# One run of key-by-query products for two pairs of heads, on all four quarters of the array

## The chip, the cores and the metric

The program runs on one core of one Trainium2 chip. The metric is the device time of one execution in microseconds (us). Three runs of the kernel before gave 384.01, 384.09 and 385.25 us; the median is 384.09.

## What is computed

The reference has two stages. The first is a linear recurrence per head (batch 4, 8 heads, 768 steps, head size 48); the second is causal attention with four experts, of which each token takes the two with the highest gate:

```python
for t in range(S):                                  # per batch and head
    cur = einsum('bhd,bhe->bhde', u[None] * kt, vt)
    y[:, :, t] = einsum('bhd,bhde->bhe', rt, state + cur)
    state = wt[:, :, :, None] * state + einsum('bhd,bhe->bhde', kt, vt)
...
logits = x @ w_gate                                 # x: y of all heads, 768 x 384 per batch
topk = argpartition(-logits, K)[..., :K]            # K = 2 of E = 4
for e in range(E):
    q, k, v = x @ wq[e], x @ wk[e], x @ wv[e]       # head size 64
    a = softmax(causal(scale * q @ k.T))
    out += (weight of e) * (a @ v @ wo[e])
```

## The kernel before

The work is cut into eight units: a batch `b` and a half `g` of its 768 steps (names carry both digits: `xp01` is batch 0, second half). Each unit has a recurrence part (`rwkv`, L325) and an attention part (`moe`).

The recurrence part goes through the eight heads as four pairs (`p`, the third digit: `aps012`). A half has six chunks of 64 steps. Per pair, DVE scans the decays backward and forward inside the chunks (`suf` L382, `pre` L386); keys and queries are multiplied with the scans (`kt` L391, `pre` L393, on DVE or POOL). Then TensorE (PE) makes four kinds of runs, all products with fp32 operands:

- `ktp` (L421): three transposes of the weighted keys, copied out as `kts`.
- `ups` (L451, L452): what each chunk adds to the state, 12 products; DVE carries the state over the chunks in a scan (`ys` L459).
- `aps` (L437): keys by queries inside each chunk, 6 chunks x 2 heads = 12 products of 64 x 64. Head 0 lies in partitions 0 to 63, head 1 in 64 to 127, and each result goes to the same half of the partitions of one PSUM bank. So two of the four 64 x 64 quarters of the array are in use. DVE masks the result (`am` L440, one instruction on 128 partitions).
- `yps` (L481, L484): the output of the pair, from the state and from `am`, 24 products; DVE adds it to `xn` (`addy`, L490).

A product shows as two matmul records in the trace, so an `aps` run has 24 records and a `yps` run 48. The records of `ktp` are one per transpose.

When the four pairs of a unit are done, `xp` (L504) transposes `xn`, and `xh` and `xl` (L506, L508) split it into two fp32r parts. The attention part starts with the projections `pp` (L550), which wait for all three `xl` of the unit, then `vp` (L573), scores `sp` (L641), row maxima `mx` (L655), exponentials `a` (L657), transposes `tp` (L671), `yp` (L699) and `op` (L767).

All products of the recurrence use the PSUM tag `rw`, which has two banks: `ktp`, `aps` and `xp` take one, `ups` and `yps` both. The attention part has two banks `mo` and two double banks `sc`.

The order of the instructions is not the order of the code. Every step is an entry in a `Plan` with the engines that could do it, a cost, a due time and the tiles it needs; `Plan.order` puts the entries on the engines one by one, by due time and readiness, and the instructions are then issued in that order. Due times are positions in the unit plus a number per kind (tables `OFF` and `OFF0`, the latter for the first unit and the constants). In the beginning 94 filler products (`warm`, L816, bf16, result unused) stand in the order of PE: 14 at the very start, 80 wherever the plan saw PE without work. Constants for the masks are made on DVE (`masks`, L293); the weights are loaded and split into two parts by ACT and DVE (`weights`, L308).

Of the kernel before, what the change touches and what calls it, by code (L numbers as in the profile page):

```python
# [51 lines left out]
class Slot:  # L52
# [6 lines left out]
    def __call__(self):  # L59
# [14 lines left out]
BOTH = {"DVE": {"suf", "pre", "ys", "kt", "mr", "uk", "ur", "ux", "yl", "wsplit", "carry", "gate", "masks"},  # L74
        "POOL": {"kt", "mr", "uk", "ur", "ux", "gate", "g4", "wsplit"}}
# [132 lines left out]
def rwkv_moe(ctx: ExitStack, tc: tile.TileContext, wkr, vY, nat, uN,  # L208
# [99 lines left out]
    def weights(n, src, cols, parts=1):  # L308

        f = sb([128, cols], F32, "ATa", f"w_{n}")  # L310
        h = cst.tile([128, cols], F32R, name=f"wh_{n}")
        l = cst.tile([128, cols], F32R, name=f"wl_{n}")
        wts[n] = (h, l)
        load("wload", f, src, cols, [f])
        for c in range(parts):
            o = slice(c * cols // parts, (c + 1) * cols // parts)
            plan.add("wsplit", {"ACT": t_act(cols // parts) + 40}, lambda e, o=o: nc.scalar.copy(h[:, o], f()[:, o]),
                     [f], [("wh", n, c)])
            plan.add("wsplit", {"DVE": t_dve(cols // parts)}, lambda e, o=o: nc.vector.tensor_tensor(
                l[:, o], f()[:, o], h[:, o].bitcast(F32), op=ALU.subtract), [f, ("wh", n, c)], [("wl", n, c)])  # L320
# [4 lines left out]
    def rwkv(b, g, v0, v1):  # L325
# [9 lines left out]

        for p in range(NP):
# [88 lines left out]
            aps = bank("rw", f"aps{n}")  # L425

# [42 lines left out]
            yps = [bank("rw", f"yps{n}{h}") for h in range(2)]  # L469

            def outp(e, yps=yps, pre=pre, am=am, ys=ys, vy=vy):

                for i in range(3):
                    for part in range(2):
                        for h in range(2):
                            o = slice(i * D, (i + 1) * D)
                            r = slice(0, 64) if h == 0 else slice(64, 64 + D)
                            for q in range(2):
                                c = 2 * i + q
                                if part == 0:  # L480
                                    nc.tensor.matmul(yps[h]()[half(q), o], pre()[r, c, 0:C], ys()[r, :, c],  # L481
                                                     start=i == 0, stop=False)
                                else:
                                    nc.tensor.matmul(yps[h]()[half(q), o], am()[half(h), c, :], vy()[half(h), c, :],  # L484
                                                     start=False, stop=i == 2)
            plan.add("yps", {"PE": T_YPS}, outp, [pre, am, ys, vy], yps, mode="q", claim=[xn])

            for h in range(2):
                def addy(e, y=yps[h], o=slice((2 * p + h) * D, (2 * p + h + 1) * D)):
                    nc.vector.tensor_tensor(xn()[:, :, o], y()[:, 0:3 * D].rearrange("p (i e) -> p i e", i=3), xn()[:, :, o],  # L490
                                            op=ALU.add)
                plan.add("addy", {"DVE": t_dve(144)}, addy, [yps[h], (xn, p, h)], [(xn, p, h)])
# [27 lines left out]
    def moe(b, g, v0, v1):  # L520
# [95 lines left out]
        def scores(ep, i):  # L616
# [30 lines left out]
            plan.add("sc", {"PE": T_SC[3 * g + i]}, mm, [qh, ql, "masks"] + [(k, gg) for k in (kh, kl) for gg in range(g + 1)],  # L647
# [59 lines left out]
        def gather(i0, i1):  # L707
# [29 lines left out]
        def weigh(ep, yp, gT, i0, i1, yr, h, l):  # L737
# [9 lines left out]
            plan.add("gb", {"PE": 56 * (i1 - i0)}, mm, [gT], [gb], mode=GMODE[1])  # L747
# [62 lines left out]
    plan.add("masks", {"DVE": 2300}, masks, [], ["masks"])  # L810
# [25 lines left out]
BUFS = dict(lt=4, nat=3, ys=2, vy=3, suf=2, pre=3, am=2, kt=2, rk=2, kts=2, xn=2, xh=2, xl=2, lg=2, asum=2, ge=2, m1=2, rank=2, c1=1, c2=1,  # L836
            gs=2, mx=6, a=4, gg=2, gT=2, g3=2, yr=2, yh0=1, yh1=1, yl0=1, yl1=1, ob=3, v_sb0=1, v_sb1=1, ATa=3, ATb=2,
# [3 lines left out]
OFF = {'ld': -29.96, 'ldn': 1.58, 'ldv': -29.15, 'wload': 16.35, 'wsplit': 10.69, 'masks': -18.45, 'ldu': 21.72, 'uk': 21.36, 'ur': 6.66, 'rk': 1.63, 'ux': -0.38, 'ktp': 2.58, 'kts': -5.41, 'aps': 4.52, 'am': -13.64, 'ups': -2.03, 'us': -28.33, 'ys': -19.09, 'carry': 4.05, 'yps': -5.57, 'addy': 7.66, 'mr': -7.19, 'suf': 7.47, 'st': 3.45, 'yl': 18.34, 'wd': -16.55, 'xh': -22.56, 'yh': -0.23, 'ql': -3.54, 'ev': 7.02, 'pre': 0.41, 'g3': 12.57, 'warm': 1.65, 'ob': 3.25, 'lg': 3.18, 'sc': 0.35, 'yr': 32.73, 'xp': -3.54, 'gate': -0.08, 'inv': -0.13, 'gT': 14.31, 'y': -10.3, 'v': -2.96, 'exp': 10.79, 'op': 1.66, 'qd': 1.09, 'xl': -6.38, 'gp': -9.61, 'kt': -4.29, 'gb': -19.78, 'tp': 1.67, 'proj': -1.5, 'av': 3.07, 'vproj': 3.81, 'max': 8.92}  # L841
T_APS, T_UPS, T_YPS = 750, 395, 890
# [73 lines left out]
```

## Time and profile before

| | us |
|---|---|
| median of 3 runs | 384.09 |
| profiled execution | 385.41 |
| its span | 383.6 |
| PE busy | 370.9 |
| DVE busy | 314.0 |
| ACT busy | 230.7 |
| POOL busy | 150.3 |

The span runs from the first to the last instruction of the profiled execution; 1.8 us lie around it. Busy times are unions of records, and the filler products count as busy PE. On PE records overlap, so what a run of products takes is read from its start to the start of the next kind, not from the length of its records.

### The profile page before, as it was taken

Reading aid. Unit: us, or ns where it says so; the run is one execution under the profiler, and the core shown is the slowest. Engines: PE = TensorE matmul, PEld = TensorE weight load, DVE = VectorE, ACT = ScalarE, POOL = GpSimd, SP = SyncE. Lnnn points to the kernel's source line nnn. Section 1 sums busy time; section 2 is a strip of 40 time slices with the busy share of each in tenths; the row PEclk is TensorE's granted clock in tenths of the full one; section 3 lists DMA queues with packets and bytes.
Section 4 is the critical chain, followed back from the end, with each engine's and each line's share of the span. In section 5 each row is a group of like instructions: output and inputs, shape, how many; then the busy total and the mean of one; then the engine's idle time right before and its main releaser. Section 6 shows DMA issues by size and latency. Waiting matters only on the chain.

```text
span 383.6 us, 12786 instructions
## 1 busy us (share of the span) xinstructions
PE 370.9 (97%) x5259; PEld 287.9 (75%) x5259; DVE 314.0 (82%) x703; ACT 230.7 (60%) x646; POOL 150.3 (39%) x264
## 2 busy tenths in 40 slices
PE   8899999999999999999999999999999999999986
PEld 3555877778868778878878778788867868878765
DVE  7998998999899999989797988699896866347563
ACT  2563566746576767365766667447564745456653
POOL 4547647462425445526331465235641401001010
PEclk9999999999999999999999999999999999999999
DMA  7987264454424543644423343244321000101001
GB/s 252 367 271 228 72 209 157 136 179 144 153 63 142 158 141 100 224 117 139 131 69 113 123 129 94 95 137 146 95 63 48 17 3 23 41 3 64 0 2 62
DMA packets 18058, 45.18 MB, mean 118 GB/s; under 512 B 2000, under 2 KB 9424, under 8 KB 18000
## 3 DMA queue, kind: packets, MB, share of 16 engines
q1 hardware_dynamic: 18000, 44.37, 36.0%
q8 instruction: 41, 0.67, 0.7%
q14 instruction: 17, 0.14, 0.1%
HBM read 39.64 MB, written 4.72 MB: 116 GB/s over the span
## 4 chain that ended last, share of the span: by engine, by line
PE 75%; DVE 14%; ACT 4%; issue 2%; DMA 2%; POOL 1%; SPq 0%; ACTq 0%; DVEq 0%; POOLq 0%
PE pp L550 11%; PE tp L671 9%; PE yp L699 9%; PE sp L641 9%; PE op L767 7%; PE vp L573 7%; PE aps L437 6%; PE yps L481 4%; PE ups L451 2%; PE ktp L421 2%; DVE mx L655 2%; PE yps L484 2%; DVE suf L382 2%; PE warm L816 2%; ACT a L657 2%
## 5 line engine op out<-in xcount | busy, mean ns | idle before, releaser
L657 ACT ACTIVATE a<-sp,mx 128x128 f32<-128x128 f32 (+5 forms) x96 | 60.6, 635 | 29.5 <-DVE mx L655 22.9
L655 DVE TENSOR_REDUCE mx<-sp 128x1 f32<-128x128 f32 (+5 forms) x96 | 56.5, 615 | 14.5 <-PE sp L646 12.7
L671 PE MATMUL tp<-ident,a 128*128 128x128 f32 x336 | 56.3, 283 | 3.0 <-ACT a L657 1.4
L671 PEld LDWEIGHTS tp<-ident,a 128*128 128x128 f32 x336 | 37.6, 140 | 11.7 <-ACT a L657 3.2
L227 ACT COPY ATa<-tp 128x512 f32<-128x512 f32 (+3 forms) x66 | 32.2, 496 | 20.2 <-PE tp L671 19.7
L391 POOL TENSOR_TENSOR kt<-lt,suf 128x384 f32<-128x384 f32 x28 | 27.5, 981 | 42.9 <-PE aps L437 16.3
L398 POOL TENSOR_TENSOR nat<-nat,u_sb 128x288 f32<-128x288 f32 x30 | 28.9, 963 | 27.7 <-DMA nat<-in_nat_dram 19.7
L699 PE MATMUL yp<-ATa,v_sb 128*64 128x384 f32 (+2 forms) x240 | 38.3, 435 | 0.0
L550 PE MATMUL pp<-xh,wh_qk 128*128 128x384 f32 x96 | 37.1, 387 | 0.0
L411 ACT ACTIVATE xn<-nat,rk 128x48 f32<-128x48 f32 x117 | 29.9, 327 | 10.4 <-DVE rk L404 10.2
L382 DVE TENSOR_TENSOR_SCAN suf<-lt,one_suf 128x390 f32<-128x390 f32 x32 | 34.2, 1072 | 1.3 <-DMA lt<-in_wkr_dram 1.2
L386 DVE TENSOR_TENSOR_SCAN pre<-lt,inv_pre 128x390 f32<-128x390 f32 x32 | 33.4, 1045 | 0.2
L389 ACT COPY wdec<-suf 128x288 f32<-128x288 f32 x32 | 22.7, 711 | 17.5 <-DVE suf L382 11.4
L393 POOL TENSOR_TENSOR pre<-lt,pre 128x384 f32<-128x384 f32 x22 | 23.2, 1055 | 24.4 <-PE sp L646 9.1
L550 PE MATMUL pp<-xl,wh_qk 128*128 128x384 f32 x96 | 32.4, 338 | 0.0
L550 PE MATMUL pp<-xh,wl_qk 128*128 128x384 f32 x96 | 32.4, 337 | 0.0
L481 PE MATMUL yps<-ys,pre 64*64 64x48 f32 (+1 forms) x768 | 31.3, 262 | 0.9 <-DVE ys L459 0.6
L459 DVE TENSOR_TENSOR_SCAN ys<-ust,wdec 112x384 f32<-112x384 f32 x32 | 30.3, 951 | 2.1 <-ACT ust L227 1.3
L437 PEld LDWEIGHTS aps<-pre,kt 64*64 64x64 f32 x768 | 24.8, 134 | 7.0 <-issue 3.5
L437 PE MATMUL aps<-pre,kt 64*64 64x64 f32 x768 | 28.5, 221 | 1.3 <-DVE xn L490 0.5
L816 PE MATMUL warm<-one_suf 128*128 128x512 bf16 x94 | 27.1, 417 | 1.4 <-POOL one_suf L247 1.4
L481 PEld LDWEIGHTS yps<-ys,pre 64*64 64x64 f32 (+1 forms) x768 | 21.2, 133 | 9.5 <-issue 3.0
(136 smaller groups left out, 947.9 us busy)
## 6 DMA issues: line engine op xcount, KB each, us to landing
lt<-in_wkr_dram SPq DMA_DIRECT2D x31, 579.5 KB, 4.0
nat<-in_nat_dram SPq DMA_DIRECT2D x32, 432.0 KB, 3.9
vy<-in_vY_dram SPq DMA_DIRECT2D x32, 144.0 KB, 2.9
out_dram<-ob SPq DMA_DIRECT2D x24, 192.0 KB, 1.9
w_qk<-in_wqk_dram SPq DMA_DIRECT2D x1, 768.0 KB, 8.1
w_vg<-in_wvg_dram SPq DMA_DIRECT2D x1, 390.0 KB, 8.7
lt<-in_wkr_dram SPq DMA_DIRECT2D x1, 384.0 KB, 5.3
w_o<-in_wo_dram SPq DMA_DIRECT2D x1, 384.0 KB, 8.6
```

What stands on the lines that cost most here:

```text
L227: nc.scalar.copy(o, i)
L382: plan.add("suf", {"DVE": t_scan(WB)}, lambda e, suf=suf, w_=w_: nc.vector.tensor_tensor_scan(rev(suf()), rev(w_()), rev(one_suf), 0.0, op ...
L386: plan.add("pre", {"DVE": t_scan(WB)}, lambda e, pre=pre, w_=w_: nc.vector.tensor_tensor_scan(flat(pre()), w_()[:, 0:WB - 1], flat(inv_pre ...
L437: nc.tensor.matmul(a_[half(h), c * C:(c + 1) * C], k[half(h), c, :], m[half(h), c, 0:C], start=True, stop=True)
L481: nc.tensor.matmul(yps[h]()[half(q), o], pre()[r, c, 0:C], ys()[r, :, c], start=i == 0, stop=False)
L550: nc.tensor.matmul(pp()[:, 0:384], w[:, qk, k, cs], x()[:, k, :], start=(k == j == 0), stop=(k == j == 2))
L641: nc.tensor.matmul(spv(x)[:, h, :], q()[p, t], flat(k())[p, o], start=j == 0, stop=j == 2 and h < np_ - 1)
L655: plan.add("max", {"DVE": t_dve(n)}, lambda e, x=x, mx=mx: nc.vector.tensor_reduce(mx(), spv(x), axis=AX.XY, op=ALU.max, negate=True), [sp ...
L657: plan.add("exp", {"ACT": t_exp(n)}, lambda e, x=x, y=y, mx=mx, a=a: nc.scalar.activation(a()[:, 0:n].rearrange("p (a n) -> p a n", a=np_) ...
L671: nc.tensor.transpose(tp()[:, j * 128:(j + 1) * 128], a()[:, (j0 + j) * 128:(j0 + j + 1) * 128], ident)
L699: nc.tensor.matmul(yp()[e * 64:e * 64 + 64, lo:hi], v_sb[ep]()[:, j, e * 64:e * 64 + 64], at, start=(j == 0), stop=(j == nj - 1))
L816: plan.add("warm", {"PE": 216}, lambda e: nc.tensor.matmul(w()[:, 0:512], wz[:, 0:128], wz, start=True, stop=True), [], [w], want=1e6 if i ...
```

## The change

1. `aps` is no longer made per pair. Every second pair makes one run for itself and the pair before it: 24 products, 48 records. The first pair's heads go to their own half of the partitions of one bank, as before; the second pair's heads go to the other half of a second bank (`half(h ^ x)`), so all four quarters are named in turn.
2. The mask of the first pair is one DVE instruction on 128 partitions as before. That of the second pair is two on 64 partitions each, since it moves each half back to where its head belongs.
3. `yps` and `addy` of both pairs are entered after that (`finish`). `kt` and `pre` have four buffers now (2 and 3 before), `a` five (4 before).
4. In the beginning, `identb` and the four pieces of `idh` are made on ACT, `idh` is cleared on POOL, the rest of the masks stays on DVE. The weight splits have due times by matrix.
5. The plan's cost of an `aps` run, and all due times, are other numbers, so the order changes everywhere.

```diff
 def masks(e):
-    nc.vector.tensor_copy(identb, ident)
-    nc.vector.memset(idh, 0.0)
+    nc.scalar.copy(identb, ident)
     for a in range(2):
         for h in range(2):
             p = slice(64 * h, 64 * h + 64)
-            nc.vector.tensor_copy(idh[p, a, 64 * a:64 * a + 64], identb[p, 64 * h:64 * h + 64])
+            nc.scalar.copy(idh[p, a, 64 * a:64 * a + 64], ident[p, 64 * h:64 * h + 64])
+
+def masks2(e):
...
-def amat(e, aps=aps, kt=kt, pre=pre):
-    a_, k, m = aps(), kt(), pre()
-    for c in range(NH):
-        for h in range(2):
-            nc.tensor.matmul(a_[half(h), c * C:(c + 1) * C], k[half(h), c, :], m[half(h), c, 0:C],
-                             start=True, stop=True)
-plan.add("aps", {"PE": T_APS}, amat, [kt, pre], [aps], mode="q", claim=[am])
-plan.add("am", {"DVE": t_dve(384)}, lambda e, am=am, aps=aps: nc.vector.tensor_tensor(
-    am(), aps()[:, 0:NH * C].rearrange("p (c j) -> p c j", j=C),
-    dec_mask[:, None, :].to_broadcast([128, NH, C]), op=ALU.mult), [aps], [am])
...
+two.append((n, kt, pre, am, finish))
+if p % 2 == 0:
+    continue
+apss = [bank("rw", f"aps{t[0]}") for t in two]
+def amat(e, two=two, apss=apss):
+    for c in range(NH):
+        for h in range(2):
+            for x, (_, kt, pre, _, _) in enumerate(two):
+                nc.tensor.matmul(apss[x]()[half(h ^ x), c * C:(c + 1) * C], kt()[half(h), c, :], pre()[half(h), c, 0:C],
+                                 start=True, stop=True)
+plan.add("aps", {"PE": T_APS}, amat, [k for t in two for k in t[1:3]], apss, mode="q", claim=[t[3] for t in two])
+for x, (_, _, _, am, _) in enumerate(two):
+    for h in range(2) if x else (None,):
+        def mask(e, x=x, h=h, am=am, aps=apss[x]):
+            o = i = slice(0, 128)
+            if x:
+                o, i = half(h), half(1 - h)
+            nc.vector.tensor_tensor(am()[o], aps()[i, 0:NH * C].rearrange("p (c j) -> p c j", j=C),
+                                    dec_mask[i, None, :].to_broadcast([i.stop - i.start, NH, C]), op=ALU.mult)
+        plan.add("am", {"DVE": t_dve(384)}, mask, [apss[x]], [(am, h)])
+for t in two:
+    t[4]()
...
-T_APS, T_UPS, T_YPS = 750, 395, 890
+T_APS, T_UPS, T_YPS = 1100, 395, 890
```

What stands where, at the three places that the prediction speaks of. First PE, in the attention part of batch 0, first half, where the products `aps010` and `aps011` of the next unit are made. Before, `aps010` stands alone, and `aps011` follows 36 rows later:

```order
L646 LDWEIGHTS idh_99
L646 MATMUL sp00000_754<-causal_100,idh_99 128x128
L646 LDWEIGHTS idh_99
L646 MATMUL sp00000_754<-causal_100,idh_99 128x128
L437 MATMUL aps010_771<-pre010_711,kt010_685 64x64 x12
L573 MATMUL vp001_786<-wh_vg_112,xh00_453 128x260
L573 MATMUL vp001_786<-wl_vg_113,xh00_453 128x260
L573 MATMUL vp001_786<-wh_vg_112,xl00_462 128x260
L573 MATMUL vp001_786<-wh_vg_112,xh00_453 128x260
L573 MATMUL vp001_786<-wl_vg_113,xh00_453 128x260
L573 MATMUL vp001_786<-wh_vg_112,xl00_462 128x260
```

Now:

```order
L596 MATMUL vp000_789<-wh_vg_113,xl00_508 128x260
L596 MATMUL vp000_789<-wh_vg_113,xh00_500 128x260
L596 MATMUL vp000_789<-wl_vg_114,xh00_500 128x260
L596 MATMUL vp000_789<-wh_vg_113,xl00_508 128x260
L501 MATMUL aps010_800<-pre010_601,kt010_539 64x64
L501 MATMUL aps011_802<-pre011_691,kt011_688 64x64
L501 MATMUL aps010_800<-pre010_601,kt010_539 64x64
L501 MATMUL aps011_802<-pre011_691,kt011_688 64x64
L501 MATMUL aps010_800<-pre010_601,kt010_539 64x64
L501 MATMUL aps011_802<-pre011_691,kt011_688 64x64
```

Products of the two pairs now alternate, for 24 rows, and three products of `vp000` and nine of `vp001` stand between them and the first `yps010`.

Second DVE, the masks of the same two pairs. Before:

```order
L459 SCALAR_TENSOR_TENSOR ys010_784<-ust0_86,wdec0_80 112x384
L440 TENSOR_TENSOR am010_798<-aps010_771,dec_mask_96 128x384
L655 TENSOR_REDUCE mx0000_806<-sp00000_754 128x1
L655 TENSOR_REDUCE mx0010_808<-sp00000_754 128x1
L579 COPY lg00_752<-vp001_786 128x4
L382 SCALAR_TENSOR_TENSOR suf012_842<-lt012_455,one_suf_66 128x390
L490 TENSOR_TENSOR xn01_590<-yps0100_811,xn01_590 128x3x48
L490 TENSOR_TENSOR xn01_590<-yps0101_814,xn01_590 128x3x48
L384 RECIPROCAL inv_pre_69<-suf012_842 128x6
L655 TENSOR_REDUCE mx0001_877<-sp00010_848 128x1
L655 TENSOR_REDUCE mx0011_883<-sp00010_848 128x1
L440 TENSOR_TENSOR am011_892<-aps011_864,dec_mask_96 128x384
```

Now:

```order
L393 SCALAR_TENSOR_TENSOR pre012_780<-lt012_388,inv_pre_69 128x390
L453 SCALAR_TENSOR_TENSOR ys011_798<-ust1_88,wdec1_83 112x384
L585 TENSOR_TENSOR Kl00_826<-pp0001_742,Kh00_787 128x384
L510 TENSOR_TENSOR am010_832<-aps010_800,dec_mask_96 128x384
L510 TENSOR_TENSOR am011_844<-aps011_802,dec_mask_96 64x384 x2
L602 COPY lg00_856<-vp000_789 128x4
L408 TENSOR_TENSOR nat013_740<-nat013_740 128x288
L602 COPY lg00_856<-vp001_837 128x4
```

The one mask of `am010` is followed at once by the two of `am011`; before, `am011` stood ten rows later.

Third DVE, the end of the first unit's recurrence, where the last two `xl00` let the first projection start. Before:

```order
L319 TENSOR_TENSOR wl_vg_113<-w_vg_272,wh_vg_112 128x780
L490 TENSOR_TENSOR xn00_228<-yps0030_597,xn00_228 128x3x48
L490 TENSOR_TENSOR xn00_228<-yps0031_600,xn00_228 128x3x48
L319 TENSOR_TENSOR wl_o_115<-w_o_287,wh_o_114 128x768
L508 TENSOR_TENSOR xl00_462<-xp001_632,xh00_453 128x384
L508 TENSOR_TENSOR xl00_462<-xp002_636,xh00_453 128x384
L404 TENSOR_REDUCE rk011_655<-nat011_520 128x6
L413 TENSOR_TENSOR xn01_590<-nat011_520,rk011_655 128x3x48
L382 SCALAR_TENSOR_TENSOR suf010_668<-lt010_355,one_suf_66 128x390
L382 SCALAR_TENSOR_TENSOR suf011_677<-lt011_384,one_suf_66 128x390
```

Now:

```order
L389 SCALAR_TENSOR_TENSOR suf011_671<-lt011_370,one_suf_66 128x390
L486 TENSOR_TENSOR xn00_294<-yps0030_639,xn00_294 128x3x48
L486 TENSOR_TENSOR xn00_294<-yps0031_642,xn00_294 128x3x48
L391 RECIPROCAL inv_pre_69<-suf011_671 128x6
L398 TENSOR_TENSOR kt011_688<-lt011_370,suf011_671 128x384
L393 SCALAR_TENSOR_TENSOR pre011_691<-lt011_370,inv_pre_69 128x390
L531 TENSOR_TENSOR xl00_508<-xp001_677,xh00_500 128x384
L531 TENSOR_TENSOR xl00_508<-xp002_682,xh00_500 128x384
L411 TENSOR_REDUCE rk012_701<-nat012_530 128x6
L325 TENSOR_TENSOR wl_vg_114<-w_vg_277,wh_vg_113 128x780
```

Both scans of `011`, its `kt` and (further up) the scans of `010` have come ahead of the last two `xl00`; `wl_vg` and `wl_o`, the low parts of two weight matrices, have gone behind it. On PE all 94 fillers now stand ahead of the first `pp`; before, 8 of them stood behind it. The transposes `ktp010` and `ktp011` now stand ahead of it too, and did not before.

## Rows read from the trace of the kernel before

**Rows 1.** The page's part 1, busy time of each engine, and the chain's part by line.

```profile
PE 370.9 (97%) x5259; PEld 287.9 (75%) x5259; DVE 314.0 (82%) x703; ACT 230.7 (60%) x646; POOL 150.3 (39%) x264
...
PE pp L550 11%; PE tp L671 9%; PE yp L699 9%; PE sp L641 9%; PE op L767 7%; PE vp L573 7%; PE aps L437 6%; PE yps L481 4%; PE ups L451 2%; PE ktp L421 2%; DVE mx L655 2%; PE yps L484 2%; DVE suf L382 2%; PE warm L816 2%; ACT a L657 2%
```

**Rows 2.** Windows of the core: length, busy time of each engine with counts, granted clock, DMA.

```profile
core 0: us, PE busy (x) PEld busy (x) DVE busy (x) ACT busy (x) POOL busy (x), PEclk, DMA share, GB/s
0.00:38.29 38.29, 35.30 (x491) 19.28 (x492) 34.23 (x77) 17.13 (x44) 19.87 (x31) 1.00 0.82 280
100.00:140.00 40.00, 38.82 (x657) 29.12 (x650) 38.71 (x75) 27.02 (x73) 18.47 (x28) 1.00 0.44 134
60.00:180.00 120.00, 118.54 (x1898) 93.88 (x1896) 111.85 (x246) 77.34 (x224) 61.20 (x92) 1.00 0.46 140
38.29:383.60 345.31, 335.65 (x4770) 268.58 (x4768) 279.77 (x627) 213.53 (x602) 130.43 (x234) 1.00 0.32 100
```

**Rows 3.** Timeline of PE, two `aps` runs: start, length, line, tiles, count, idle before.

```profile
45.45 0.92 PE L437 MATMUL aps<-pre,kt 64*64 64x64 f32 x24
46.29 0.39 PE L573 MATMUL vp<-wh_vg,xh 128*128 128x260 f32 x1
...
174.89 1.61 PE L437 MATMUL aps<-pre,kt 64*64 64x64 f32 x48
176.43 0.39 PE L573 MATMUL vp<-wh_vg,xh 128*128 128x260 f32 x1
```

**Rows 4.** Timeline of PE, one `ups` run from first product to next kind.

```profile
44.20 0.25 PE L451 MATMUL ups<-nat,kts 64*64 64x48 f32 x1
...
44.72 0.33 PE L641 MATMUL sp<-Kh,Qh 64*128 64x128 f32 x2
```

**Rows 5.** Timeline of PE, one `yps` run from first product to next kind.

```profile
18.29 0.38 PE L481 MATMUL yps<-ys,pre 64*64 64x48 f32 x8
...
19.27 0.39 PE L816 MATMUL warm<-one_suf 128*128 128x512 bf16 x1
```

**Rows 6.** Timeline of PE, last fillers, first projection, one `ktp` run.

```profile
36.75 1.89 PE L816 MATMUL warm<-one_suf 128*128 128x512 bf16 x8
38.29 0.52 PE L550 MATMUL pp<-xh,wh_qk 128*128 128x384 f32 x1
...
41.89 0.52 PE L421 MATMUL ktp<-ident,kt 128*128 128x128 f32 x3
42.24 0.38 PE L816 MATMUL warm<-one_suf 128*128 128x512 bf16 x1
```

**Rows 7.** Timeline of DVE at the start: masks, first scans, one `am`.

```profile
3.45 0.23 DVE L294 CAST identb<-ident 128x128 bf16<-128x128 f32 x1
...
6.22 0.96 DVE L382 TENSOR_TENSOR_SCAN suf<-lt,one_suf 128x390 f32<-128x390 f32 x1
8.43 0.97 DVE L382 TENSOR_TENSOR_SCAN suf<-lt,one_suf 128x390 f32<-128x390 f32 x1 [1.25 <-DMA lt<-in_wkr_dram]
...
14.81 0.54 DVE L440 TENSOR_TENSOR am<-aps,dec_mask 128x384 f32<-128x384 f32 x1
15.28 0.56 DVE L401 TENSOR_TENSOR nat<-nat 128x288 f32<-128x288 f32 x1
```

**Rows 8.** Groups of DVE, 6.2 to 38.3 us: busy, mean ns, idle before.

```profile
L386 DVE TENSOR_TENSOR_SCAN pre<-lt,inv_pre 128x390 f32<-128x390 f32 x4 | 4.9, 1232 | 0.1
L382 DVE TENSOR_TENSOR_SCAN suf<-lt,one_suf 128x390 f32<-128x390 f32 x4 | 4.3, 1065 | 1.2 <-DMA lt<-in_wkr_dram 1.2
L319 DVE TENSOR_TENSOR wl_o<-w_o,wh_o 128x768 fp32r<-128x768 f32 x1 | 1.2, 1189 | 0.0
L319 DVE TENSOR_TENSOR wl_vg<-w_vg,wh_vg 128x780 fp32r<-128x780 f32 x1 | 1.0, 961 | 0.0
L384 DVE RECIPROCAL inv_pre<-suf 128x6 f32<-128x6 f32 x4 | 0.7, 175 | 0.0
```

**Rows 9.** Group of PE, line L437: busy, mean ns, idle before and what ended it.

```profile
L437 PE MATMUL aps<-pre,kt 64*64 64x64 f32 x768 | 28.5, 221 | 1.3 <-DVE xn L490 0.5 <-DVE pre L393 0.4 <-DVE ust L229 0.3
```

More of the change, by code (lines that the diff above doesn't have):

```diff
@@ L70 @@
          "SP": dict(PE=2000, DVE=2000, ACT=2000, POOL=2000, SP=2000)}
-BOTH = {"DVE": {"suf", "pre", "ys", "kt", "mr", "uk", "ur", "ux", "yl", "wsplit", "carry", "gate", "masks"},
-        "POOL": {"kt", "mr", "uk", "ur", "ux", "gate", "g4", "wsplit"}}
+BOTH = {"DVE": {"suf", "pre", "ys", "kt", "mr", "uk", "ur", "ux", "yl", "wsqk", "wsvg", "wso", "carry", "gate", "masks"},
+        "POOL": {"kt", "mr", "uk", "ur", "ux", "gate", "g4"}}
 class Plan:
@@ L316, in weights @@
             o = slice(c * cols // parts, (c + 1) * cols // parts)
[L317 removed]
+            plan.add("ws" + n, {"ACT": t_act(cols // parts) + 40}, lambda e, o=o: nc.scalar.copy(h[:, o], f()[:, o]),
                      [f], [("wh", n, c)])
[L319 removed]
+            plan.add("ws" + n, {"DVE": t_dve(cols // parts)}, lambda e, o=o: nc.vector.tensor_tensor(
                 l[:, o], f()[:, o], h[:, o].bitcast(F32), op=ALU.subtract), [f, ("wh", n, c)], [("wl", n, c)])
@@ L334, in prod @@
             return {"DVE": t_dve(cols), "POOL": t_pool(cols)} if first or FLEX else {"POOL": t_pool(cols)}
+        two = []
         for p in range(NP):
@@ L467, in rwkv @@
                          [], [ku + ("in",)])
[L469 to L492, printed above, removed]
+            def finish(p=p, n=n, pre=pre, am=am, ys=ys, vy=vy):
+                want(p / (NP + 1))
+                yps = [bank("rw", f"yps{n}{h}") for h in range(2)]
+                def outp(e, yps=yps, pre=pre, am=am, ys=ys, vy=vy):
+                    for i in range(3):
+                        for part in range(2):
+                            for h in range(2):
+                                o = slice(i * D, (i + 1) * D)
+                                r = slice(0, 64) if h == 0 else slice(64, 64 + D)
+                                for q in range(2):
+                                    c = 2 * i + q
+                                    if part == 0:
+                                        nc.tensor.matmul(yps[h]()[half(q), o], pre()[r, c, 0:C], ys()[r, :, c],
+                                                         start=i == 0, stop=False)
+                                    else:
+                                        nc.tensor.matmul(yps[h]()[half(q), o], am()[half(h), c, :], vy()[half(h), c, :],
+                                                         start=False, stop=i == 2)
+                plan.add("yps", {"PE": T_YPS}, outp, [pre, ys, vy] + [(am, h) for h in ((0, 1) if p % 2 else (None,))], yps, mode="q", claim=[xn])
+                for h in range(2):
+                    def addy(e, y=yps[h], o=slice((2 * p + h) * D, (2 * p + h + 1) * D)):
+                        nc.vector.tensor_tensor(xn()[:, :, o], y()[:, 0:3 * D].rearrange("p (i e) -> p i e", i=3), xn()[:, :, o],
+                                                op=ALU.add)
+                    plan.add("addy", {"DVE": t_dve(144)}, addy, [yps[h], (xn, p, h)], [(xn, p, h)])
@@ L494, in rwkv @@
+            for t in two:
+                t[4]()
+            two = []
         want(NP / (NP + 1))
@@ L646, in mm @@
                         nc.tensor.matmul(spv(x)[:, np_ - 1, w - 128:w], idh[p, a, :], causal[p, a, :], start=False, stop=a == 1)
-            plan.add("sc", {"PE": T_SC[3 * g + i]}, mm, [qh, ql, "masks"] + [(k, gg) for k in (kh, kl) for gg in range(g + 1)],
+            plan.add("sc", {"PE": T_SC[3 * g + i]}, mm, [qh, ql, "masks", "masks1"] + [(k, gg) for k in (kh, kl) for gg in range(g + 1)],
                      sps, mode="r")
@@ L809, in rwkv_moe @@
     plan.now = -1.0
-    plan.add("masks", {"DVE": 2300}, masks, [], ["masks"])
+    plan.add("masks", {"ACT": 600}, masks, [], ["masks1"])
+    plan.add("masks2", {"DVE": 1400}, masks2, [], ["masks"])
     plan.add("ldu", {"SP": 475}, lambda e: nc.sync.dma_start(
@@ L835 @@
 FLEX, LATE, SLACK = (True, True, 125)
-BUFS = dict(lt=4, nat=3, ys=2, vy=3, suf=2, pre=3, am=2, kt=2, rk=2, kts=2, xn=2, xh=2, xl=2, lg=2, asum=2, ge=2, m1=2, rank=2, c1=1, c2=1,
-            gs=2, mx=6, a=4, gg=2, gT=2, g3=2, yr=2, yh0=1, yh1=1, yl0=1, yl1=1, ob=3, v_sb0=1, v_sb1=1, ATa=3, ATb=2,
+BUFS = dict(lt=4, nat=3, ys=2, vy=3, suf=2, pre=4, am=2, kt=4, rk=2, kts=2, xn=2, xh=2, xl=2, lg=2, asum=2, ge=2, m1=2, rank=2, c1=1, c2=1,
+            gs=2, mx=6, a=5, gg=2, gT=2, g3=2, yr=2, yh0=1, yh1=1, yl0=1, yl1=1, ob=3, v_sb0=1, v_sb1=1, ATa=3, ATb=2,
             sc=2, mo=2, rw=2)
```

19 lines of the change are left out of this document (11 added, 8 removed).

## The prediction

> **What bounds the kernel now.** I read the page's busy times first, then the windows, then single runs on the timelines of PE and DVE. The page shows PE busy for 97% of the span and DVE for 82%, and the chain that ended last lies on PE for most of its length [rows 1]. That share would mislead in the first 38 us, where the fillers count as work, so the windows come next. From the first projection at 38.29 us [rows 6] to the end, PE is busy 335.65 of 345.31 us, and the granted clock is 1.00 there, its upper level of 2.4 GHz [rows 2]. Ahead of it DVE is the engine that has real work: 34.23 of 38.29 us, and of the 4.1 us that it idles 1.25 are one wait for data near the beginning [rows 2, 7]. DVE stays close behind afterwards: 93% from 60 to 180 us (111.85 of 120), 97% from 100 to 140 (38.71 of 40) [rows 2]. So there are two regimes. What DVE does ahead of the last `xl` of the first unit moves everything behind it; after that, a microsecond less of products on PE is a microsecond of time, as long as DVE keeps up.
>
> **The sum is made against the profiled execution**, 385.4 us with a span of 383.6; the median of the runs is 1.3 below it, and that is taken off at the end.
>
> **The fused runs.** An `aps` run alone occupies PE for 0.84 us (45.45 to 46.29); two back to back take 1.54 (174.89 to 176.43) [rows 3]. 28 of the 32 runs lie behind the first projection; by the order 20 stand alone and 8 in four adjacent pairs: 20 x 0.84 + 4 x 1.54 = 23.0 us. They become 14 runs of 48 records. No row shows such a run, so it is bounded. It can't be shorter than today's run, since each quarter still takes 12 records: 0.84. It has no reason to be longer than two back to back: 1.54. Two runs that already use four quarters lie between: `ups`, 24 records in 0.52 (44.20 to 44.72) [rows 4], is 1.04 for 48; `yps`, 48 records, takes 0.98 (18.29 to 19.27) [rows 5]. Both stream 48 columns per record where `aps` streams 64; if all of it grew with the columns, that would be 1.39 and 1.31. I take 1.1, above `yps` by part of the columns. 14 x 1.1 = 15.4, so PE is given back 7.6 us; with 0.84 it is 11.2, with 1.39 3.5.
>
> The `yps` run starts its 48 records 20 ns apart (0.98 / 48) [rows 5]. A rule of the Trainium skill says otherwise: "TensorE: Matmul & The Clock Gate" (section "Wait — 56ns, not 53.3ns?") states that products never start closer than about 25 ns apart. By it 48 records take at least 1.2 us, an estimate, and the gain is at most 6.2 us. The trace does not agree with it, and the sum keeps the 1.1.
>
> **The masks on DVE.** An `am` record is 0.54 long and the next starts 0.47 behind it [rows 7]. The second pair's mask becomes two instructions of as many columns each, so at 0.47 apiece 16 are added, 14 of them behind the first projection: 6.6 us on DVE. From 60 to 180 us some six fused runs fall (14 over the 286 us to the last `aps`). There PE could be done 6 x 0.54 = 3.2 us sooner (23.0 - 15.4 over 14 is 0.54 each), in 116.8; DVE would need 111.85 + 2.8 = 114.65, a share of 98%. The best that the trace shows is the 97% of 100 to 140 us, which makes it 118.4, or 1.6 lost again. With a little for waits at other places I put +2.5; it could be nothing, since DVE is at 81% over the whole of 38.29 to 383.6 [rows 2], or the 8 us of the first rival.
>
> **The start.** By the order, the first unit's DVE work up to its last `xl` gains two `suf`, two `pre`, two reciprocals, a `kt`, an `rk`, three products into `xn` and two more masks, and loses `wl_o`, `wl_vg` and a copy. By the mean records of that stretch [rows 8]: 2 x 1.07 + 2 x 1.23 for the scans, 3 x 0.47 for `kt` and two masks, about 0.3 each for the six narrower ones (an estimate between the 0.18 of a reciprocal and the 0.47 of a mask), together 7.8; off go 1.19 + 0.96 for the weights and 0.47 for the copy, 2.6. That is +5.2, less some 0.4 by which records overlap. DVE is idle for 4.1 us of the first 38.29 [rows 2], 1.25 of it for the second scan's transfer, the rest ahead of its first instruction and in short waits; more work at hand can fill one or two of these. I take +3.5, from 1 to 5: the first projection at about 41.8. Part comes back: two `ktp` of 0.35 each (41.89 to 42.24) [rows 6] are done by then, -0.7, and the 8 fillers that stood behind the first projection, at 0.19 each (36.75 to 38.29 for eight) [rows 6], are gone, -1.5. The scans done early relieve DVE by their 4.6 us between 38 and 60 us, which is why no wait is added there.
>
> **The other edits.** `identb` and `idh` leave DVE, but the first scan follows the masks at 6.22 and the second still waits until 8.43 for its transfer [rows 7], so they give 0.2 at most. On ACT and POOL they lie ahead of the first scan's result, which both engines need for their first work; without that cover five copies at the 0.23 of `identb` [rows 7] would cost 1.2. `wl_vg` is needed by `vp`, behind 18 projections; `wl_o` much later: nothing. SP issues the same transfers in nearly the same order; the third scan's decays have moved ahead of one `nat` and two smaller loads, worth something between -1 and +1 inside the start's range. `finish` puts `yps` behind both pairs: in the order at least eleven attention products stand between each fused run behind the start and its first `yps`, and more again ahead of the second, against one mask of 0.47 and then two; nothing as long as DVE's queue is not late by more than these products take.
>
> Sum: 385.4 - 7.6 + 2.5 + 3.5 - 0.7 - 1.5 - 0.2 = 381.4 for a profiled execution, 380.1 for the timed ones.
>
> **Rivals.**
>
> *The fused run waits for the second pair.* It needs `kt` and `pre` of two pairs and both `rw` banks at once, and what is behind it on PE is attention work that was ready. Until the last mask has read them, neither `ktp`, `ups`, `xp` nor `yps` gets a bank. For it: DVE at 93 to 97% makes `pre`, and a late scan would now stop PE where before it stopped a quarter of its work. Against it: all 32 runs together waited only 1.3 us before [rows 9], and `kt` and `pre` have more buffers. Each 0.1 us per run beyond my 2.5 costs 1.4; from 0.3 per run it decides and the gain is gone. At 0.6 per run, 8.4 us in place of the 2.5, the time is 386.0.
>
> *The quarters don't overlap.* Then the change does not do what it says: 14 x 1.54 = 21.6, a gain of 1.4 where I have 7.6, and as PE is no faster, DVE is not pressed (the 2.5 goes): 383.8. For it: in the new run two products that share rows of the array, and then two that write the same bank, follow each other at once. Against it: today's run has 24 records in 0.84, and they already send both row halves into one bank; `yps` has twice as many in 0.98 [rows 3, 5].
>
> "TensorEngine Tiling (Array Packing)" of the Trainium skill (Gotcha 1) has a rule that would bring this about: different row tiles cannot access the same PSUM bank at the same time. By it today's run of two quarters would gain nothing from the second; the rows of `aps` and `yps` above show no such halving, so I give it little.
>
> *All of it, and more.* The fused run takes the 0.98 of `yps` (gain 9.3), DVE is never late, and the start costs 2: 385.4 - 9.3 + 2 - 2.4 - 1.3 = 374.4. For it: PE waits little now, 9.7 us from 38.29 on with the tail included [rows 2]. Against it: the wider columns, and the 97% of DVE.
>
> **How the numbers follow.** My forecast, 377 to 383, gets 0.47; the third rival 0.20; the wait for the second pair 0.20; quarters that don't overlap 0.13. The likeliest is 380.1. A range from 374.4 to 386.5 holds all but the ends of the outer cases. What a measurement of this kernel can tell from no change is about 0.3%, 1.2 us. The forecast and the third rival are faster (0.67); half of the case of no overlap and a quarter of the waiting case come out within it (0.12); the rest is slower (0.21).
>
> **What would show it.** In the profile of the changed kernel: an `aps` run of 48 records of about 1.1 us from its start to the next kind (0.85 and 1.5 are the rivals' numbers); 48 `am` records with those on 64 partitions no shorter than 0.5; the first `pp` near 41.8 us; no `warm` behind it; DVE at 95% or more from 60 to 180 us; idle time ahead of the `aps` records of less than 3 us in all. The forecast is wrong if the first `pp` comes at 38 or 45, if PE's idle time behind it grows by more than 6 us, or if the granted clock falls below 1.00 in a pause between the last filler and the first projection, which no row of before shows.

## The result, and the profile after

The change is faster, by 1%: 380.96 us median against 384.40, ratio 0.9901, 95% interval [0.9878, 0.9924]. Predicted were 380.1, and 374.4 to 386.5. The execution that was profiled then was a disturbed one of 1098.69 us (the other three took 380.67 to 381.22), so the profile after, and what the experiments are compared with, is of the same kernel run again: median 381.93 (384.74 before), ratio 0.9932 [0.9915, 0.9948]; profiled 381.39, span 379.6. For a profiled execution the sum had 381.4.

Nearly the same number, but not from the same terms. First the page of after, its part 1 and the chain by line [rows 1], and the PE and DVE groups of the two edited steps (busy, mean ns, idle before) [rows 9]:

```profile
PE 361.6 (95%) x5259; PEld 280.8 (74%) x5259; DVE 319.7 (84%) x717; ACT 237.0 (62%) x662; POOL 136.0 (36%) x254
...
PE pp L573 12%; PE yp L722 10%; PE tp L694 10%; PE sp L664 8%; PE op L790 7%; PE vp L596 6%; PE yps L477 5%; DVE am L510 3%; DVE mx L678 3%; DVE ys L453 3%; PE ups L445 2%; PE ktp L428 2%; DMA nat<-in_nat_dram 2%; DVE pre L393 2%; ACT a L680 2%
...
L510 DVE TENSOR_TENSOR am<-aps,dec_mask 64x384 f32<-64x384 f32 (+1 forms) x48 | 26.5, 552 | 1.4 <-PE aps L501 0.7
```

```profile
L501 PE MATMUL aps<-pre,kt 64*64 64x64 f32 x768 | 15.0, 222 | 0.0
```

`aps` has left the chain's first lines and `am` has come in. PE gave back 9.3 us of busy time and the span got 4.0 shorter; the rest turned into idle time. The windows, with the columns of [rows 2]:

```profile
0.00:38.29 38.29, 34.33 (x488) 17.88 (x491) 34.16 (x72) 19.81 (x55) 17.46 (x31) 1.00 0.78 274
40.00:47.00 7.00, 5.86 (x42) 4.93 (x43) 5.96 (x13) 3.25 (x8) 2.20 (x3) 0.51 0.64 196
47.00:60.00 13.00, 13.00 (x249) 11.34 (x247) 11.94 (x28) 7.17 (x21) 7.77 (x10) 1.00 0.44 133
60.00:180.00 120.00, 116.11 (x1876) 93.03 (x1875) 114.11 (x256) 80.67 (x237) 59.52 (x98) 1.00 0.45 139
```

DVE (the third busy time) is at 95% from 60 to 180 us, from 93%, and PE fell from 118.54 to 116.11 there. And the second row has what before had nowhere: a granted clock of 0.51, the lower level (1.2 GHz), for seven microseconds.

The fused run in the steady part, on PE's timeline (start, length) [rows 3]: 48 records, and the next kind starts 0.86 us after the first.

```profile
99.84 0.93 PE L501 MATMUL aps<-pre,kt 64*64 64x64 f32 x48
100.70 0.66 PE L694 MATMUL tp<-ident,a 128*128 128x128 f32 x4
```

The start, on the same timeline [rows 6]: the last fillers, the idle time behind them, and the first projection, still at the lower clock.

```profile
36.86 0.61 PE L840 MATMUL warm<-one_suf 128*128 128x512 bf16 x2
...
40.60 1.54 PE L527 MATMUL xp<-ident,xn 128*128 128x128 f32 x6 [1.89 <-DVE xn L486]
42.69 0.90 PE L428 MATMUL ktp<-ident,kt 128*128 128x128 f32 x3 [0.54 <-DVE xl L531]
43.24 0.67 PE L573 MATMUL pp<-xh,wh_qk 128*128 128x384 f32 x1
```

To see where PE's time went, each record is counted from its start to the start of the next, less the idle time between (over 30 ns), and added up by kind. Profiled executions, us; E5, E9 and E10 are experiments, below:

| | before | after | E5 | E9 | E10 |
|---|---|---|---|---|---|
| `aps` | 26.6 | 14.0 | 14.1 | 25.7 | 25.6 |
| `yps` | 32.4 | 34.1 | 34.4 | 32.4 | 31.9 |
| `tp` | 43.7 | 45.8 | 46.0 | 44.9 | 44.8 |
| `vp` | 28.9 | 30.7 | 30.7 | 30.6 | 30.6 |
| all kinds | 370.7 | 361.3 | 361.1 | 369.8 | 369.5 |
| idle, in all | 7.8 | 13.2 | 11.2 | 6.9 | 5.1 |
| idle behind the first `pp` | 6.2 | 8.1 | 7.8 | 4.5 | 3.8 |

After against before: `aps` gave 12.6; idle time took 5.3 of it back, `tp` 2.1, `yps` and `vp` 1.8 each; `yp` and others gave 2.4 more.

### The profile page after: what moved, and what is told of

It reads as the page before. It is cut to its first block, busy times and chain, and to the rows that moved or that the text cites. A ratio compares the mean times of both kernels' runs of the same rounds, so it can differ in the third digit from the quotient of the medians.

```text
span 1096.9 us, 12800 instructions
## 1 busy us (share of the span) xinstructions
PE 1087.8 (99%) x5252; PEld 677.6 (62%) x5259; DVE 322.1 (29%) x717; ACT 241.1 (22%) x662; POOL 131.2 (12%) x254
## 4 chain that ended last, share of the span: by engine, by line
PE 99%; issue 0%; DVE 0%; POOL 0%; ACT 0%; POOLq 0%
PE pp L573 17%; PE tp L694 13%; PE yp L722 13%; PE sp L664 10%; PE vp L596 8%; PE op L790 8%; PE warm L840 8%; PE yps L477 4%; PE ktp L428 4%; PE aps L501 4%; PE yps L480 3%; PE xp L527 3%; PE sp L669 2%; PE ups L446 2%; PE ups L445 1%; PE gb L768 1%
## 5 line engine op out<-in xcount | busy, mean ns | idle before, releaser
L694 PE MATMUL tp<-ident,a 128*128 128x128 f32 x336 | 154.6, 650 | 0.0
L722 PE MATMUL yp<-ATa,v_sb 128*64 128x384 f32 (+2 forms) x240 | 120.6, 1221 | 0.0
L573 PE MATMUL pp<-xh,wh_qk 128*128 128x384 f32 x96 | 90.7, 945 | 0.0
L840 PE MATMUL warm<-one_suf 128*128 128x512 bf16 x87 | 85.2, 1235 | 5.3 <-issue 3.2
L573 PE MATMUL pp<-xl,wh_qk 128*128 128x384 f32 x96 | 84.6, 881 | 0.0
L573 PE MATMUL pp<-xh,wl_qk 128*128 128x384 f32 x96 | 83.8, 873 | 0.0
L480 PE MATMUL yps<-vy,am 64*64 64x48 f32 x768 | 55.7, 368 | 0.0
L480 PEld LDWEIGHTS yps<-vy,am 64*64 64x64 f32 x768 | 53.2, 337 | 0.0
L664 PE MATMUL sp<-Kl,Qh 64*128 64x384 f32 (+4 forms) x128 | 51.0, 796 | 0.0
L664 PE MATMUL sp<-Kh,Ql 64*128 64x384 f32 (+4 forms) x128 | 49.8, 777 | 0.0
```

The lines of the kernel that those rows point to most:

```text
L573: nc.tensor.matmul(pp()[:, 0:384], w[:, qk, k, cs], x()[:, k, :], start=(k == j == 0), stop=(k == j == 2))
L664: nc.tensor.matmul(spv(x)[:, h, :], q()[p, t], flat(k())[p, o], start=j == 0, stop=j == 2 and h < np_ - 1)
L694: nc.tensor.transpose(tp()[:, j * 128:(j + 1) * 128], a()[:, (j0 + j) * 128:(j0 + j + 1) * 128], ident)
L722: nc.tensor.matmul(yp()[e * 64:e * 64 + 64, lo:hi], v_sb[ep]()[:, j, e * 64:e * 64 + 64], at, start=(j == 0), stop=(j == nj - 1))
L840: plan.add("warm", {"PE": 216}, lambda e: nc.tensor.matmul(w()[:, 0:512], wz[:, 0:128], wz, start=True, stop=True), [], [w], want=1e6 if i ...
```

## Experiments

All run in the changed order, but for E6 and E7, and all with the kernel before beside them on the same chip. Its median lay between 384.55 and 384.78 on each of these chips, so the medians of different experiments are compared below.

**E1, two quarters.** Undoes the use of the quarters alone: both pairs' heads to their own halves, masks still 1 + 2.

```diff
-    nc.tensor.matmul(apss[x]()[half(h ^ x), ...
+    nc.tensor.matmul(apss[x]()[half(h), ...
...
-            o, i = half(h), half(1 - h)
+            o, i = half(h), half(h)
```

> The changed kernel in its own order, but the second pair's products go to the same halves as the first's, so that 48 records use two quarters instead of four; its two masks stay, on the half where the result now lies. If the four quarters overlap and PE is what counts: the run grows to about 1.5 us, 14 x 0.4 = +5 to +7 us, 386 to 388. If the quarters never overlapped: no change, 381. If DVE holds the pace in the first half: the run grows, but only half of it shows, +2 to +3.

Measured 385.93, ratio to before 1.0030 [1.0016, 1.0044]: 4.0 above the changed kernel, nearest to the first expectation and short of its 5 to 7. The run's length doubles; in the first unit it is 1.59 us from its start to the filler behind it:

```profile
32.33 1.66 PE L501 MATMUL aps<-pre,kt 64*64 64x64 f32 x48
33.92 0.82 PE L840 MATMUL warm<-one_suf 128*128 128x512 bf16 x3
```

So the four quarters work side by side, and they are worth 4.0 us of the end (E9 repeats this with the clock kept up), though they take 16 x 0.73 = 11.7 us off PE's runs. Without them, but with the split masks, the change as a whole would have gained nothing.

**E2, two quarters and one mask.** As E1, and the second pair's mask is one instruction on 128 partitions, which two quarters allow.

```diff
-        if x:
-            o, i = half(h), half(1 - h)
+        if x and h:
+            return
```

> As the kernel on two quarters, but the second pair's mask is one instruction on 128 partitions again (the other entry of the plan issues nothing): 16 masks of 0.47 less, 7.5 us of DVE. If DVE had reserve: within 1 us of the kernel on two quarters. If DVE holds the pace: 2.5 us or more below it.

Measured 382.87, ratio 0.9959 [0.9943, 0.9975]: 3.1 us below E1, for 16 masks fewer, as expected if DVE holds the pace. Not all of that need be the masks: the mean granted clock of an execution was 0.990 to 0.996 in E1 and 0.990 to 1.000 in E2. With the clock kept up it is 1.7 (E9, E10). The kernel of E2 is also 1.9 us below the kernel before, on two quarters and with as many masks; the changed kernel is only 0.9 below E2, and their intervals overlap. So more than half of the gain of 2.8 stands without the four quarters. Which of the other edits gives it (order, start, buffers) no run separates; the new tables alone do not (E6).

**E3, masks twice.** The changed kernel, each half mask of the second pair issued two times.

```diff
-        nc.vector.tensor_tensor(am()[o], ...
+        for _ in range(2 if x else 1):
+            nc.vector.tensor_tensor(am()[o], ...
```

> The changed kernel, with both masks of the second pair issued twice in a row: 32 instructions of 0.47 more, 15 us of DVE in the same order. If DVE is in reserve and only the beginning is bound by it: +1 us for the beginning and +1 to +3 behind it, 383 to 385. If DVE holds the pace up to 180 us: its share there is in excess of 98% already, so +6 to +9 us, 387 to 390.

Measured 400.96, ratio 1.0411 [1.0380, 1.0442], above both expectations: 19 us for 32 more masks, more than the 15 us that 32 steps of 0.47 put on DVE. Part of the 19 is the clock, which in this profile was at its lower level for 17.75 us in three stretches, against 7 in the changed kernel; at E5's 2.6 us for seven the 10.75 us more are worth some 4 us, an estimate:

```profile
42.50:49.50 7.00, 6.24 (x44) 5.31 (x45) 5.66 (x11) 3.06 (x9) 2.92 (x3) 0.51 0.65 211
73.25:80.25 7.00, 6.70 (x75) 4.94 (x77) 4.84 (x12) 3.57 (x13) 1.58 (x2) 0.51 0.17 44
162.00:165.75 3.75, 3.75 (x103) 3.25 (x96) 3.12 (x10) 2.71 (x10) 1.28 (x4) 0.54 0.17 46
```

The largest part is idle PE before records of one kind, put down to the masks (0.4 us there in the changed kernel):

```profile
L477 PE MATMUL yps<-ys,pre 48*64 48x48 f32 (+1 forms) x768 | 36.6, 265 | 11.7 <-DVE am L511 9.7 <-DVE xl L532 1.1 <-DVE xn L486 0.6
```

Most of it stands inside the runs, behind the fourth record: 12 of the 16 `yps` runs of a first pair stop there, so that the fifth record starts 0.39 to 1.67 us after the fourth. E12 shows why.

**E5, fillers.** The changed kernel with 13 more fillers in the first unit: 8 ahead of its second `xp`, 5 behind the third (`fill` issues that many).

```diff
...
+    fill(8 if k == 1 else 0)
     for i in range(3):
         nc.tensor.transpose(xp()[:, i * 128:(i + 1) * 128], ...
+    fill(5 if k == 2 else 0)
```

> The changed kernel with 13 more filler products of 512 columns in the first unit: eight ahead of its second triple of transposes and five behind the third, where TensorE stood idle for 1.9 and 0.5 us and the granted clock was 0.5 from 40.1 to 46.9 us. Theory A (the drop of the clock costs the start what its stretch at half the clock shows): the granted clock stays at 1.00 from 33 us on, the seventeen units of work of TensorE between 40 and 47 us end about 2 to 3 us sooner, and the kernel ends 2 to 3 us before 381.9, at 379 to 380. Theory B (behind 40 us VectorE is what TensorE waits for, so the clock is hidden): the clock stays up too, the idle time of TensorE between 41 and 60 us grows by as much as its work gets shorter, and the end moves by under 0.5 us. Theory C: the fillers themselves hold up the transposes by 0.2 us each time and the time rises by 0.5 us or more.

Measured 379.36, ratio 0.9858 [0.9846, 0.9871], 2.6 us below the changed kernel and the fastest of all. The clock stays at its upper level and PE is busy throughout, in the window that had 0.51:

```profile
40.00:47.00 7.00, 7.00 (x82) 5.42 (x81) 6.70 (x15) 4.36 (x11) 3.59 (x4) 1.00 0.65 213
```

The first projection comes 0.6 sooner (42.61), that of the second unit 2.0 (72.9 after 74.9), the end of the span 2.2: won by then and kept. Theory A.

**E6, new tables alone, and E7, old tables.** The kernel before with the changed offsets and start times; the changed kernel with those of before. Of the tables one line stands here, as E7 changes it; E6 does the opposite, and `OFF`, `OFF0` and `LEAD` go with it.

```diff
-T0, T1 = (18.33, 15.35)
+T0, T1 = (21.06, 16.77)
```

> The kernel before with the changed one's table of offsets and start times, and with its own products, masks and buffers. Theory A (the gain of the change is mostly the order that the new table gives, since two quarters with one mask came out 1.9 us below the kernel before): this one ends near 382.9, 1 to 2 us below the kernel before. Theory B (the table fits only the paired products): it ends at 384.5 or above. What it can't show is the start, because it keeps its constants on VectorE: first projection between 38 and 40 us.

> The changed kernel with the offsets and start times of the kernel before: the paired products on four quarters, split masks and ScalarE's constants alone. Theory A (most of the gain is the order): 384 us or above. Theory B (most of it is the paired products, 10.3 us of TensorE's work, whose worth does not hang on the table): 382 or below.

Measured 390.30, ratio 1.0144 [1.0127, 1.0160], and 389.27, ratio 1.0115 [1.0083, 1.0147]. Theory A of E6 and theory B of E7 both fall: the new tables gain nothing with the old products, nor the fused run with the old tables. E6's clock stayed up. E7's did not, so its 389.27 is not the price of the order alone:

```profile
38.75:49.25 10.50, 8.71 (x106) 7.40 (x98) 8.07 (x17) 5.56 (x16) 6.53 (x7) 0.51 0.43 126
72.75:80.00 7.25, 7.25 (x79) 4.55 (x79) 5.26 (x14) 4.88 (x18) 3.89 (x5) 0.53 0.41 125
```

In this execution (392.09) that is 10.75 us more at the lower level than in the changed kernel, again some 4 us by E5's price (an estimate); without them it would still be above the kernel before. That each table suits its own products also limits E1, E2, E9 and E10: their order was made for four quarters.

**E8, constants on DVE.** `identb` and `idh` back on DVE, the rest of the order kept.

```diff
-    nc.gpsimd.memset(idh, 0.0)
...
-    nc.scalar.copy(identb, ident)
...
 def masks2(e):
+    nc.vector.tensor_copy(identb, ident)
+    nc.vector.memset(idh, 0.0)
...
-            nc.scalar.copy(idh[p, a, 64 * a:64 * a + 64], ident[p, 64 * h:64 * h + 64])
+            nc.vector.tensor_copy(idh[p, a, 64 * a:64 * a + 64], identb[p, 64 * h:64 * h + 64])
```

> The changed kernel with the constants identb and idh made on VectorE again, in the place of the second step, as in the kernel before; the rest of the order as it is. Theory A (VectorE sets the start, to the last subtraction of the first unit): about 1.0 us more of VectorE's work ahead of the first projection, which moves from 43.2 to about 44, and the end by 0.5 to 1 us, to 382.5 or 383. Theory B (ScalarE's constants only shift the wait): the first projection stays within 0.3 us of 43.2 and the end within 0.5 us of 381.9.

Measured 382.72, ratio 0.9950 [0.9937, 0.9963]. The first projection moves by 0.86 to 44.10, the number of theory A; the end by 0.8, but its interval overlaps that of the changed kernel, so for the end it is unclear. The way there, in the profiled execution, is not theory A's. The first scan starts 0.79 later (6.63 after 5.84), but the next one then waits less for its transfer, and the first `pre` scan starts only 0.23 later (9.38 after 9.15). What sets the start back again is PE: its first `ktp` also comes later, behind 2.15 us of idle time, the clock is at its lower level just behind that, and DVE waits for `ups`, 2.00 us where it waited 0.8 (windows, then DVE's timeline):

```profile
8.75:12.25 3.50, 3.50 (x11) 1.83 (x12) 3.45 (x6) 1.07 (x2) 0.52 (x1) 0.51 1.03 411
```

```profile
14.20 0.42 DVE L229 COPY ust<-ups 112x144 f32<-112x144 f32 x1 [2.00 <-PE ups L447]
```

**E9 and E10, the first two with the fillers.** E5 with the edit of E1, and with that of E2.

> The version with 13 more fillers, with the paired products on two quarters instead of four and both half masks kept, so that against that version only TensorE's runs differ (1.59 us for 0.86, sixteen times; 10.3 us behind the first projection). The output isn't changed. Without the fillers two quarters cost 4.0 us (385.9 against 381.9), while the clock's drop in the start was shorter in the two-quarter kernel. Theory A (that drop masked part of the worth of the quarters): 386 or a little under, since the fillers have less to give back here, and the difference to 379.4 is 6 to 7 us. Theory B (the fillers give the same 2.6 us everywhere): 383.3, the difference stays 4.

> The same with two quarters and one mask of 128 partitions for the second pair, as two quarters allow. Theory A (VectorE's 16 fewer masks are worth 3 us here too, and the clock has less to give back): 382 to 383, so that four quarters with split masks are worth 3 us net. Theory B (additive): 380.3, and the four quarters are worth 0.9 us net, as without the fillers.

Measured 383.77, ratio 0.9980 [0.9968, 0.9992], and 382.12, ratio 0.9937 [0.9920, 0.9954]. With the clock kept up the quarters are worth 4.4 us (E9 to E5), the second half mask costs 1.7 (E10 to E9), and the fused run on four quarters with its split mask is ahead of two quarters with one mask by 2.8, where without fillers it was 0.9, within the noise (E2). The kernel of E10 itself, without the four quarters, is 2.5 below the kernel before. For E9 the truth lies nearer to theory B, for E10 to theory A.

From E9 to E5 the runs of `aps` get 11.6 us shorter. By the table, 4.3 of it becomes idle PE, 2.0 goes into `yps`, 1.1 into `tp`; the span gets 4.4 shorter. Seen from DVE, in the group of the masks, E9 first:

```profile
L510 DVE TENSOR_TENSOR am<-aps,dec_mask 64x384 f32<-64x384 f32 (+1 forms) x48 | 25.1, 550 | 4.7 <-PE aps L501 4.4
```

```profile
L510 DVE TENSOR_TENSOR am<-aps,dec_mask 64x384 f32<-64x384 f32 (+1 forms) x48 | 26.4, 551 | 1.4 <-PE aps L501 0.7
```

With two quarters DVE waited 4.4 us for `aps`; with four it hardly waits, and PE waits more.

**E11, sooner.** E5 with the last two `addy` of the first unit ahead of a scan of the second unit, the last two `xl` ahead of its `pre` (and ahead of a copy and a product of the second unit), and 4 fillers for 8.

```diff
...
+    for kind, last in (("wd", xl3), ("mr", xl3), ("pre", xl3), ("suf", adds[1])):
+        i = done.index(last)
+        j = max(x for x in range(i) if done[x]["kind"] == kind)
+        done.insert(i, done.pop(j))
```

> The version with more fillers, in which VectorE's last two additions of the first unit stand ahead of the second unit's suf scan instead of behind it, the last two subtractions ahead of its pre scan, ScalarE's copy of that suf behind the casts, and four fillers instead of eight ahead of the transposes. Theory A (the start is bound by VectorE up to the last subtraction): the transposes begin at 39.7 instead of 40.6, the first projection at 41.8 instead of 42.6, and the end moves by 0.5 to 0.9 us, to 378.5 to 378.9. Theory B (what stands ahead of the first projection is only moved behind it, and the second unit's products come as much later): the first projection comes sooner but the end stays within 0.3 us of 379.4.

Measured 379.83, ratio 0.9879 [0.9856, 0.9902]; its first projection came at 43.12, not at 41.8. In that execution DVE was already 0.67 us later than in E5 at the `pre` scan before (36.77 after 36.10), then a product into `nat` (L408) took 0.99 us instead of 0.43, and the additions came at 40.24, after 39.89 in E5 and not before. Neither theory was tested; a miss.

**E12, states first.** E5, with the 24 records of a `yps` run that use the state ahead of the 24 that use the mask.

```diff
-    for i in range(3):
-        for part in range(2):
+    for part in range(2):
+        for i in range(3):
```

> The version with more fillers; in each run of output products (yps) the 24 products with the states now all stand ahead of the 24 with the masked array, where before eight of the one kind and eight of the other took turns, so that a run can be half done before it needs the second half mask. In the version with more fillers the 32 runs of this kind take 34.4 us in all, against 31.9 where one mask serves both halves and none of them waits; the longest wait inside a run stands behind its first four records. Theory A (these waits for the half masks, 2.0 to 2.5 us, are part of what the split costs): the runs fall back to about 32 us and the end moves by 1 to 2 us, to 377.5 to 378.5. Theory B (VectorE itself is the bound there, so the wait only moves to the next run that needs VectorE): the runs get shorter by 2 us, the waits ahead of other runs grow by as much, and the end stays within 0.5 us of 379.4.

Measured 380.11, ratio 0.9886 [0.9870, 0.9903]: no gain, and the `yps` runs did not get shorter (35.2 us). Both theories had the wrong wait. In E12 no product with the mask stands among the first 24 records, yet the run still stops behind its fourth record, for 0.23 us here, and goes on at 51.995. Timeline of PE:

```profile
51.66 0.98 PE L477 MATMUL yps<-ys,pre 64*64 64x48 f32 x22
52.38 0.23 PE L480 MATMUL yps<-vy,am 64*64 64x48 f32 x2
```

And of DVE, the masks:

```profile
50.14 1.71 DVE L510 TENSOR_TENSOR am<-aps,dec_mask 128x384 f32<-128x384 f32 x3 [0.25 <-PE aps L501]
```

The last half mask ends at 50.14 + 1.71 = 51.85. The order, with the waits of each instruction, says which one it is; `yps_871` and `yps_874` are the two banks of this run:

```
L477 MATMUL yps_871<-ys_761,pre_601 64x48 [waits DVE_49]
L477 MATMUL yps_871<-ys_761,pre_601 64x48
L477 MATMUL yps_874<-ys_761,pre_601 64x48 [waits DVE_49,PE_49]
```

The third product, record five, is the first into the second `rw` bank. That bank holds the second pair's products until both half masks have read it. In E12 the program puts `yps_874` where the second pair's `aps` was, and the count of DVE instructions that its first product waits for is the one that the last half mask raises. So the first pair's output waits for the second pair's masks: not for their data, but for the bank. In the changed kernel four of the 16 `yps` runs of a first pair stop there behind a mask: the fifth record starts 0.20 to 0.48 us after the fourth, and 0.08 where nothing is waited for. In the kernel before one run did (0.32).

## Why the prediction came out

The bounds that it named held in the main: DVE up to the last `xl`, then PE with DVE close behind. Its steps, one by one.

- **The fused run** was taken at 1.1 us and measures 0.86, close to the lower bound of 0.84, the length of one run of two quarters [rows 3]. The failed step is "above `yps` by part of the columns": 64 columns cost no more here than the 48 of `yps` (0.99 now). 14 x 0.86 = 12.0 makes the term -11.0 where the sum had -7.6. 48 records in 0.86 us start 18 ns apart on average. The least distance of about 25 ns that the Trainium skill ("TensorE: Matmul & The Clock Gate", section "Wait — 56ns, not 53.3ns?") states for products is no bound for these, which lie on four quarters.
- **Quarters that don't overlap** is out by E1. (By the order, products that follow each other there write the two banks in turn; it is every second one that writes the same bank, from the other row half, and not the next as the prediction has it.) Two row halves write one bank throughout that run, so Gotcha 1 of "TensorEngine Tiling (Array Packing)" in the Trainium skill does not show here, where they write different partitions.
- **The start** was too small: first projection at 43.24, not 41.8. E5, whose clock stays up, has it at 42.61, so 0.6 of the miss is the clock. The other 0.8 is idle time: I let the added work fill DVE's idle time, and DVE still idles 4.1 of its first 38.29 us. The constants on ACT, put at 0.2, are not refuted: E8 has 0.86 at the first projection, but DVE's own part of it is 0.23, and the rest came by way of PE and its lower clock.
- **The 8 fillers** counted as -1.5 for being gone from behind the first projection, and 2.0 us of PE's time there are gone. What failed is what the step left out: with all 94 used by 37.5 us, PE stood idle for 1.9 us and the granted clock was at its lower level from 40 to 47. E5 prices that at 2.6 us. It was named as what would prove the forecast wrong, and it had no term in the sum. By that sign the forecast's account failed here, though its number held.
- **The masks** cost more than +2.5. Their 48 records at 0.55 and the 95% of DVE were as forecast, and idle time ahead of `aps` is nil. But idle PE behind the first projection grew by 1.9 and the `yps` runs there got 1.5 longer. The idle time is in the attention part, ahead of `vp` (1.2 more, put down to ACT), `gb` (1.2) and `yp` (0.7, both put down to DVE), less what `aps` and others no longer wait. The `yps` runs stop for the bank, mostly too briefly to show as idle time ahead of a record. E3 and E12 show that mechanism: it is that of the first rival, both `rw` banks held until the masks have read them. Beyond the 2.5 the two are 0.9 / 14, under 0.1 us per run, below the 0.3 from which it decides; E3 is where it does.

Term by term, in us, from the profiled executions and counted like the table above, behind the first projection alone (all rows but the first):

| | in the sum | measured |
|---|---|---|
| first projection | +3.5 | +4.95 |
| `aps` | -7.6 | -10.95 |
| `warm` | -1.5 | -2.0 |
| `ktp` | -0.7 | -1.9 |
| idle PE and `yps` | +2.5 | +3.4 |
| other edits | -0.2 | not seen apart |
| `vp` and `tp` | none | +3.9 |
| `yp` and other kinds | none | -1.4 |
| sum | -4.0 | -4.0 |

The terms were off by up to 3.9 us and cancelled: that the sum came out to the tenth is luck. The lower clock has no row of its own; it lies in the first projection, and in the projections behind it, which E5 has 1.2 shorter. What stays open is `vp` and `tp`, 1.8 and 2.1 us longer than before: `vp` is so in E9 and E10 too, and half of `tp`, so that much comes with the new order and not with the quarters; no run tells more.

## What to carry to other kernels

Before joining two steps into one, ask which buffers the joint step holds, and until which reader: here a bank that the next step needed first was held until the longer masks had read it, and the `yps` runs got 1.8 us longer; with the masks doubled it was the larger part of the loss. Time saved on an engine at 97% is worth its full price only until the second engine, at 93%, is the bound: of 11.6 us 4.4 came through. Where fillers hold up the clock, moving the first real work later needs more of them: 13 were worth nearly as much as the change itself. An experiment that delays PE's work can also lower the clock; its price is the edit's own only where the clock stayed up.

## What was not expected of the hardware

- Four 64 x 64 quarters on fp32 operands take no longer than two: 48 records in 0.86 us against 24 in 0.84, although both halves of the rows write each of the two banks.
- A pause of 1.9 us, up to 40.60, and then only transposes (1.54 us for six, against 0.82 in E5): the granted clock was at its lower level for seven us (0.51 from 40 to 47), nearly four of them behind the first projection at 43.24.
- A DVE mask on 64 partitions costs what one on 128 does: 0.55 us each in E9's and E10's groups of 48 and 32.
